# Attention and two feed-forward stages on one core: a port in the task order, low halves of weights by unit, conversions from unit index 3, earlier opening products

## Chip, core and metric

The kernel runs on one core of a Trainium2 chip. The metric is the device time of one execution in microseconds (us), from several runs; a profile shows one execution, engine by engine. The engines are called TensorE (PE; its weight loads are PEld), VectorE (DVE), ScalarE (ACT), GpSimd (POOL) and SyncE (SP, which issues the DMAs here).

## What is computed

```
attn = softmax(rot(q) @ rot(k).T / 8) @ v            # 2 batches, 8 heads, 576 x 64
x    = attn as (1152, 512)
x    = sum over e of p[:, e] * (relu(x @ w1[e]) @ w2[e])   # 4 experts, 512 -> 1024 -> 512
h    = x @ w_in;  out = max(0.01 * h, h) @ w_out           # 512 -> 2048 -> 512
```

All inputs and the output are fp32 in value; w_in and w_out reach the kernel as 64-bit words and are turned into fp32 by it.

## The kernel before

Products run in a reduced fp32 form: each operand is split into a rounded high half and the rest (low half), and three of the four products of halves are added. So each weight and each activation needs a rounding (`rounded`, L261) and a subtraction (`sub`, L908, recorded as L909).

The kernel has two parts, each with an order of instructions that a small list scheduler (`Plan`, L80) works out when the program is built: a task has a list of engines that may run it, a price on each, a rank, and the tasks it waits for. `Plan.order` goes through time, lets the engine that is free earliest take its ready task of lowest rank, and adds a lag for the signal; the instructions are issued in that order on each engine. `Plan({...})` gives the time at which each engine comes free from the part before. On the chip the engines run their queues in order and wait on semaphores, so the planned times set only the order.

The first part is attention, with half of the work of the first three units for block 0 mixed in. The second (from L843) runs twelve units of 512 hidden columns: units 0 to 7 are the four experts, two each; 8 to 11 are the second feed-forward stage. The 1152 tokens are two blocks: block 0 of 512, block 1 of 640. Units 0 to 2 (`AHEAD = 3`) have only block 1 left, the others both.

A unit has two stages. Stage 1 makes the hidden values by a seven-product scheme per quad (a block and a half of the columns): seven sums or plain quarters of the first matrix (`W1`, A11, A12, A22, S1 to S4, in `weights1`, L931) meet quarters, differences and sums of x (`x_sums`, `x_differences`, L983 to L995). Product 1 and product 5 open a quad, each in a bank of four called `start`; `seeded` (L1039) copies a bank into the next by ScalarE (L1042), `add_fifth` (L1045) adds product 5 by VectorE, and `hidden` (L997) empties a bank: high half on ScalarE (L1003), low half on VectorE (L1004). Unit 0 uses plain products (`stage1_whole`, L1013, recorded as L522). Stage 2 multiplies the hidden values by the second matrix (`W2`, `weights2`, L960), twelve matmuls for each tile of 128 tokens (L467), in a `start` bank, and VectorE adds the result to `acc` (L542, L545). Behind unit 7, `turned` (L1104) transposes `acc` into the x of the second stage, and its quarters and differences are split (L1098 to L1100).

Weights come in by `load_w` (L922) through three raw buffers of 512 KB, in turn. `converted` (L966) turns one piece of w_in or w_out (32 pieces, to be used from unit 8 on) into fp32: a load into one of two `wide` buffers, two steps on ScalarE (L974, L975), two on VectorE (L976, L977), one on GpSimd (L978), one on VectorE (L979), and a store to `narrow`. Pieces are ranked by planned time, 32 in 300 us, from unit 0 on.

Today the low halves and sums of weights may go to VectorE or GpSimd, whichever comes free first with a handicap; high halves to ScalarE or GpSimd.

Of the kernel before, what the change touches and what calls it, by code (L numbers as in the profile page):

```python
# [11 lines left out]
F32 = mybir.dt.float32  # L12
# [8 lines left out]
P = 128  # L21
# [9 lines left out]
HOLD = 3.5  # L31
# [36 lines left out]
LAG = {"PE": 0.2, "ACT": 0.16, "DVE": 0.19, "POOL": 0.12, "SP": 0.65, "DMA": 2.4}  # L68
# [11 lines left out]
class Plan:  # L80
# [18 lines left out]
    def order(self):  # L99
        free, ready, done, order, missing = dict(self.start), {}, {}, [], list(self.missing)  # L100

        def arrive(i):
            for e, us, more in self.tasks[i][1]:
                ready.setdefault(e, []).append((at[i], self.tasks[i][2] + more, i, us))

        at = [0.0] * len(self.tasks)
# [3 lines left out]
        while len(order) < len(self.tasks):  # L110
# [10 lines left out]
            _, _, i, us = min((x for x in ready[e] if x[0] <= t), key=lambda x: (x[0], x[2]) if e == "DMA" else x[1:3])  # L121
# [35 lines left out]
def attention_then_two_ffns(ctx, tc, xqk, vp, rope, dprob, w1, w2, w_in, w_out, out):  # L157
# [464 lines left out]
    with tc.manual_schedule():  # L622
# [230 lines left out]
        raw = [raw_p.tile([P, 2, FU], F32, name=f"raw{i}") for i in range(3)]  # L853
# [5 lines left out]
        wide = [cv_p.tile([P, FU, 2], I32, name=f"wide{i}") for i in range(2)]  # L859
# [8 lines left out]
        plan = Plan({"ACT": 7.5, "DVE": 12, "PE": 11})  # L868
        written, read = {}, {}

        def do(fn, choices, rank, reads=(), writes=(), also=()):
# [7 lines left out]
            t = plan.add(fn, [(c[0], c[1], c[2] if len(c) > 2 else 0) for c in choices], after, rank)  # L879
# [9 lines left out]
        def moved(fn, kb, rank, reads=(), writes=()):  # L889

            t = do(lambda e: fn(), [("SP", 0.48)], rank, reads, writes)
            d = plan.add(lambda e: None, [("DMA", kb / 260, 0)], [t], rank)
            for s in reads:
                read[s].append(d)
            for s in writes:
                written[s] = [d]
            return d

        def on(n, **more):
            return [(e, {"ACT": 0.15 + n / 1200, "DVE": 0.13 + n / 960}[e], x) for e, x in more.items()]  # L900

        def pair(n, **more):
            return [(e, {"DVE": 0.1 + n / 960, "POOL": 0.2 + n / 465}[e], x) for e, x in more.items()]

        def round_(n, **more):
            return [(e, {"ACT": 0.15 + n / 1200, "POOL": 0.2 + n / 1180}[e], x) for e, x in more.items()]
# [4 lines left out]
        def halves(name, hi, lo, x, n, rank, reads, slot, first=None, second=None):  # L911

            do(lambda e: rounded(e, hi, x), round_(n, **(first or {"POOL": 0, "ACT": 2})), rank, reads, [slot])
            do(sub(lo, x, f32(hi)), pair(n, **(second or {"POOL": 0, "DVE": 3})), rank, list(reads) + [slot], [slot])

        spin = {"raw": 0, "start": 0, "g": 0, "fifth": 0}

        def turnof(what, n):
            spin[what] += 1
            return (spin[what] - 1) % n  # L920

        def load_w(u, which, rank):  # L922
            rs = []
            for j in range(2):
                r = turnof("raw", len(raw))
# [3 lines left out]
            return rs  # L929

        def weights1(u, due):  # L931
# [5 lines left out]
            use = {"first": {"ACT": 0, "POOL": 0}, "second": {"POOL": 0, "DVE": 0}} if whole_ else {"first": {"ACT": 0, "POOL": 1}}  # L937
# [22 lines left out]
        def weights2(u, due):  # L960
            rs = load_w(u, 1, due)
            for c in range(NC):
                x = raw[rs[c // 2]][:, c % 2]
                halves(f"w2_{c}", W2[c][:, 0], W2[c][:, 1], x, 512, due + .5 * c, [("raw", rs[c // 2])], ("w2", c))

        def converted(i, due):  # L966
# [5 lines left out]
            w = ("wide", k)  # L972
            moved(lambda: sp.dma_start(raw_.rearrange("p f w -> p (f w)"), wide_weights(j, which)[:, c]), 512, due - 12, (), [w, ("low", k)])
            do(lambda e: act.activation(t, low.bitcast(U32), AF.Copy, scale=2.0 ** -29), [("ACT", 0.65)], due, [w, ("low", k)], [("rest", k)])  # L974
            do(lambda e: act.activation(s, high.bitcast(F32), AF.Square), [("ACT", 0.65)], due, [w], [("sq", k)])  # L975
            do(lambda e: dve.tensor_scalar(low, high, 3, 0x3FFFFFFF, op0=ALU.logical_shift_left, op1=ALU.bitwise_and), [("DVE", 0.85)], due, [w], [("low", k)])  # L976
# [232 lines left out]
```

## Time and profile before

| | us |
|---|---|
| median of 3 runs | 785.78 (785.42 to 786.85) |
| the profiled execution | 783.96 |
| its span, first to last instruction | 782.10 |
| TensorE busy in it | 734.7 (94%) |
| VectorE busy | 552.9 (71%) |
| GpSimd busy | 458.2 (59%) |
| ScalarE busy | 395.1 (51%) |

Times in the rows count from the first instruction of the profiled execution. The page splits the span into 40 slices of 19.6 us, with a digit for the busy tenths of each engine. A matmul's end is modelled, and successive ones overlap, so a group's duration is a little longer than the distance to the next group; distances are used for prices.

### The profile page before, as it was taken

The numbers are of one execution on the slowest core, as the hardware profiler recorded it, in microseconds if no ns is written. First come the engines' busy times: TensorE is split into PE (matmuls) and PEld (weight loads), VectorE is DVE, ScalarE is ACT, GpSimd is POOL, SyncE is SP. The second block draws the span as 40 slices with busy tenths as digits, with TensorE's granted clock in tenths as the row PEclk, the third lists the DMA queues.
The fourth block names the chain that finished last, engine by engine and source line by source line (L and its number), as shares of the span: only waits on it lengthen the run. The fifth ranks groups of instructions, "written<-read, shape, count | busy, mean of one in ns | idle before, by whom it ended". The sixth has DMA issues, their size and how long they took to land.

```text
span 782.1 us, 12238 instructions
## 1 busy us (share of the span) xinstructions
PE 734.7 (94%) x4396; PEld 658.2 (84%) x4396; DVE 552.9 (71%) x914; ACT 395.1 (51%) x964; POOL 458.2 (59%) x452
## 2 busy tenths in 40 slices
PE   6789899999998789599999999999997999999998
PEld 6678778888887678589898998989887889898997
DVE  6998977788758999977698785735569546264442
ACT  5688885766544464447263562504336427063450
POOL 7877957655249978748365383412558618265340
PEclk9999999999999999999999999999998999999999
DMA  8666645544024562555464543201101101020002
GB/s 264 173 199 154 156 109 130 165 120 106 14 96 135 136 215 80 162 183 168 148 180 142 167 151 115 96 27 55 54 1 55 54 30 52 27 78 5 1 28 95
DMA packets 40813, 84.57 MB, mean 108 GB/s; under 512 B 4656, under 2 KB 9520, under 8 KB 40752
## 3 DMA queue, kind: packets, MB, share of 16 engines
q1 hardware_dynamic: 39936, 83.00, 35.6%
q10 hardware_dynamic: 816, 0.79, 0.3%
q8 instruction: 35, 0.57, 0.3%
q14 instruction: 26, 0.21, 0.1%
HBM read 60.64 MB, written 10.75 MB: 91 GB/s over the span
## 4 chain that ended last, share of the span: by engine, by line
PE 72%; DVE 14%; POOL 5%; issue 3%; DMA 3%; ACT 2%; SPq 1%; POOLq 0%; ACTq 0%; DVEq 0%
PE start L467 30%; PE seeded L515 15%; PE start L515 10%; PE hy L467 4%; PE hp L588 4%; PE s L307 3%; PE o L467 3%; PE t L390 2%; DVE w L909 2%; DVE tmp L909 2%; DMA x<-in_xqk_dram 2%; DVE nm L324 1%; DVE pt L419 1%; POOL tmp L909 1%; DVE wide L977 1%
## 5 line engine op out<-in xcount | busy, mean ns | idle before, releaser
L467 PE MATMUL start<-w,h 128*128 128x512 f32 (+1 forms) x1164 | 269.8, 389 | 5.9 <-DVE h L1004 5.9
L467 PEld LDWEIGHTS start<-w,h 128*128 128x128 f32 x1164 | 215.1, 188 | 49.7 <-DVE h L1004 7.1
L515 PE MATMUL seeded<-xT,w 128*128 128x320 f32 (+1 forms) x480 | 74.9, 307 | 12.5 <-ACT seeded L1042 12.5
L515 PEld LDWEIGHTS seeded<-xT,w 128*128 128x128 f32 x480 | 70.3, 198 | 14.2 <-ACT seeded L1042 13.5
L978 POOL TENSOR_TENSOR rest<-wide,rest 128x512 int32<-128x512 int32 x32 | 45.2, 1413 | 61.1 <-DVE wide L977 27.2
L545 DVE SCALAR_TENSOR_TENSOR acc<-start,prob,acc 128x512 f32<-128x512 f32 x55 | 41.1, 748 | 54.4 <-PE start L467 54.3
L515 PE MATMUL seeded<-xt,w 128*128 128x320 f32 (+1 forms) x480 | 74.7, 302 | 0.0
L265 POOL TENSOR_SCALAR w<-raw 128x512 fp32r<-128x512 f32 x38 | 28.0, 737 | 78.7 <-PE start L467 67.9
L515 PE MATMUL start<-xT,w 128*128 128x320 f32 (+1 forms) x480 | 73.4, 298 | 0.1
L515 PEld LDWEIGHTS seeded<-xt,w 128*128 128x128 f32 x480 | 69.6, 194 | 0.9 <-ACT seeded L1042 0.3
L515 PEld LDWEIGHTS start<-xT,w 128*128 128x128 f32 x480 | 67.5, 190 | 1.5 <-DVE g L1009 0.3
L415 ACT ACTIVATE pt<-t 128x384 fp32r<-128x384 f32 (+2 forms) x128 | 53.4, 440 | 26.0 <-PE t L390 22.9
L909 POOL TENSOR_TENSOR h<-g,h 128x256 fp32r<-128x256 f32 (+1 forms) x64 | 55.2, 883 | 19.2 <-ACT h L1010 19.1
L419 DVE TENSOR_TENSOR pt<-t,pt 128x384 fp32r<-128x384 f32 (+2 forms) x128 | 60.1, 491 | 8.8 <-ACT pt L415 7.2
L1042 ACT ACTIVATE seeded<-start 128x320 f32<-128x320 f32 (+1 forms) x40 | 16.0, 399 | 93.4 <-PE start L515 40.8
L307 PE MATMUL s<-stk 128*128 128x288 f32 x288 | 53.3, 315 | 8.2 <-ACT p L334 5.4
L909 POOL TENSOR_TENSOR w<-raw,w 128x512 fp32r<-128x512 f32 x39 | 58.5, 1506 | 3.4 <-ACT w L263 2.4
L334 ACT ACTIVATE p<-s,nm 128x576 f32<-128x576 f32 x72 | 53.3, 740 | 12.8 <-DVE nm L324 12.2
L909 DVE TENSOR_TENSOR w<-raw,w 128x512 fp32r<-128x512 f32 x46 | 51.2, 1142 | 7.4 <-ACT w L263 5.2
L324 DVE TENSOR_REDUCE nm<-s 128x1 f32<-128x576 f32 x72 | 53.6, 749 | 3.9 <-PE s L307 3.1
L549 DVE TENSOR_TENSOR acc<-start,acc 128x512 f32<-128x512 f32 (+1 forms) x28 | 18.8, 673 | 51.7 <-PE start L467 51.7
L390 PE MATMUL t<-ident,p 128*128 128x128 f32 x288 | 45.6, 276 | 9.5 <-ACT p L334 3.7
(140 smaller groups left out, 1450.2 us busy)
## 6 DMA issues: line engine op xcount, KB each, us to landing
raw<-in_w_dram SPq DMA_DIRECT2D x32, 512.0 KB, 3.8
wide<-in_w_in_dram SPq DMA_DIRECT2D x16, 512.0 KB, 4.4
narrow<-rest SPq DMA_DIRECT2D x32, 256.0 KB, 4.0
wide<-in_w_out_dram SPq DMA_DIRECT2D x16, 512.0 KB, 3.8
raw<-narrow SPq DMA_DIRECT2D x16, 512.0 KB, 3.7
x<-in_xqk_dram SPq DMA_DIRECT2D x14, 576.0 KB, 6.6
stk<-hl SPq DMA_DIRECT2D x28, 288.0 KB, 5.5
hraw<-in_w_dram SPq DMA_DIRECT2D x12, 512.0 KB, 4.2
```

Source lines behind the costliest of these rows:

```text
L307: pe.matmul(sc[:, c, :HS], lhsT=l, rhs=r[:, c * HS:(c + 1) * HS], start=(k == 0), stop=(k == len(ops) - 1))
L324: dve.tensor_reduce(out=NM[n], in_=SC[n][:, :, :HS], axis=AX.XY, op=ALU.max, negate=True)
L334: act.activation(PP[p, i][:, h].rearrange("p (c k) -> p c k", c=2), SC[n][:, :, :HS], AF.Exp, bias=NM[n], accum_out=SM[p][:, col:col + 1])
L390: pe.transpose(t[:, j], flat[:, b * P:(b + 1) * P], ident)
L415: act.activation(hi, src, AF.Copy)
L419: dve.tensor_tensor(out=lo, in0=src, in1=f32(hi), op=ALU.subtract)
L467: pe.matmul(ps, lhsT=l, rhs=r, start=(k == 0), stop=(k == len(ops) - 1))
L515: pe.matmul(out, lhsT=W1[a][:, l, c, fs], rhs=x_of(g, b, r, c), start=first and (c, k) == (0, 0), stop=(c, k) == (1, 2), skip_group_check= ...
L545: dve.scalar_tensor_tensor(out=acc, in0=ps, scalar=prob[:, t, e:e + 1], in1=acc, op0=ALU.mult, op1=ALU.add)
L588: pe.matmul(HP[v, f], lhsT=w[:, c, l, f * P:(f + 1) * P], rhs=x[:, r, c], start=(c, k) == (0, 0), stop=(c, k) == (NC - 1, 2))
L909: return lambda e: eng[e].tensor_tensor(out=o, in0=a, in1=b, op=op)
L978: do(lambda e: pool.tensor_tensor(out=t, in0=low, in1=t, op=ALU.add), [("POOL", 1.45)], due, [w, ("low", k)], [("rest", k)])
```

## The change

- `Plan.order` knows a resource "port": a task that is marked (all two-input operations between buffers on VectorE and GpSimd, GpSimd's roundings, the conversion's steps) starts no earlier than the last marked task ended. Tasks that are free at the start count from -15 us, and SyncE and the DMA engines are free from there. A pseudo-engine "X" marks when the last attention results for block 1 are there (8.5 us).
- Low halves and sums of weights run on VectorE alone in units 0 to 3, 8 and 9 (`ON_DVE`), on GpSimd alone in the others; unit 0's first matrix keeps its choice. High halves of weights run on ScalarE alone.
- Two more raw buffers take the place of the two `wide` ones; units 0 to 2 and 8 to 11 load through all five, units 3 to 7 through three, and conversions use the other two.
- Conversions are added from unit index 3 on, eight per unit in units 3 to 6.
- Products 1 and 5 of the next unit's first quad are added ahead of stage 2 of the unit before, with a rank 3 us into it (behind unit 7: after its stage 2); the bank of product 1 is held until product 2 has been added to it, and the other tiles use the remaining banks. `HOLD` for the last tile is 0.
- The sums of x for block 1 run on GpSimd, those for block 0 on VectorE; differences and low halves of x on VectorE, high halves on ScalarE. For the second stage they are ranked in the order in which products need them.

The core of the diff:

```diff
-HOLD = 3.5
+HOLD = 0
+EARLY = 3
+ON_DVE = (0, 1, 2, 3, 8, 9)
...
+            for e, us, more, *port in self.tasks[i][1]:
+                ready.setdefault(e, []).append((at[i], self.tasks[i][2] + more, i, us, any(port)))

+        at = [-15.0] * len(self.tasks)
...
+            if port:
+                t = max(t, free.get("port", 0.0))
+                free["port"] = t + us
...
-        raw = [raw_p.tile([P, 2, FU], F32, name=f"raw{i}") for i in range(3)]
+        raw = [raw_p.tile([P, 2, FU], F32, name=f"raw{i}") for i in range(5)]
+        wide = [r.bitcast(I32).rearrange("p c f -> p (c f)").rearrange("p (f w) -> p f w", w=2) for r in raw[3:]]
...
-        wide = [cv_p.tile([P, FU, 2], I32, name=f"wide{i}") for i in range(2)]
...
-        plan = Plan({"ACT": 7.5, "DVE": 12, "PE": 11})
+        plan = Plan({"POOL": 0.0, "ACT": 7.5, "DVE": 12, "PE": 11, "SP": -15.0, "DMA": -15.0})
...
+            return [(e, {"DVE": 0.16 + n / 960, "POOL": 0.2 + n / 465}[e], x, True) for e, x in more.items()]
+            return [(e, {"ACT": 0.2 + n / 1200, "POOL": 0.2 + n / 1180}[e], x, e == "POOL") for e, x in more.items()]
...
-            do(lambda e: rounded(e, hi, x), round_(n, **(first or {"POOL": 0, "ACT": 2})), rank, reads, [slot])
-            do(sub(lo, x, f32(hi)), pair(n, **(second or {"POOL": 0, "DVE": 3})), rank, list(reads) + [slot], [slot])
+            do(lambda e: rounded(e, hi, x), round_(n, **(first or {"ACT": 0})), rank, reads, [slot])
+            do(sub(lo, x, f32(hi)), pair(n, **(second or {"DVE": 0})), rank, list(reads) + [slot], [slot])
...
+        held = set()
+
         def turnof(what, n):
+            while (what, spin[what] % n) in held:
+                spin[what] += 1
             spin[what] += 1
             return (spin[what] - 1) % n
...
-                r = turnof("raw", len(raw))
+                r = turnof("raw", 5 if u < AHEAD or u >= 2 * E else 3)
...
+        def LOW(u):
+            return {"DVE": 0} if u in ON_DVE else {"POOL": 0}
...
-            use = {"first": {"ACT": 0, "POOL": 0}, "second": {"POOL": 0, "DVE": 0}} if whole_ else {"first": {"ACT": 0, "POOL": 1}}
+            use = {"first": {"ACT": 0, "POOL": 0}, "second": {"POOL": 0, "DVE": 0}} if whole_ else {"second": LOW(u)}
...
-                    do(sub(t[o], x, y, f), pair(n, POOL=0, DVE=0.5), due + i, reads, [("tmp", o)])
+                    do(sub(t[o], x, y, f), pair(n, **LOW(u)), due + i, reads, [("tmp", o)])
...
-                halves(f"w2_{c}", W2[c][:, 0], W2[c][:, 1], x, 512, due + .5 * c, [("raw", rs[c // 2])], ("w2", c))
+                halves(f"w2_{c}", W2[c][:, 0], W2[c][:, 1], x, 512, due + .5 * c, [("raw", rs[c // 2])], ("w2", c), second=LOW(u))
...
+        LATE = {B11: 0, T1: 1, T2: 2, B21: 3, T3: 4, B22: 5, T4: 6}
+        XD = [4, 8]
...
+                do(sub(tmp[2 * k + h][:, :, :n], f32(x_block(g, i, 0)), f32(x_block(g, i, 1)), ALU.add), pair(2 * n, **({"POOL": 0} if g else {"DVE": 0})), due, [("x", g, i)], [("tmp", 2 * k + h)])
...
-                do(sub(t[o], t[x], t[y]), pair(2 * n, DVE=0, POOL=0), due, slots, [("tmp", 2 * o[0] + o[1])])
+                do(sub(t[o], t[x], t[y]), pair(2 * n, DVE=0), due + LATE[i] * (due > 100), slots, [("tmp", 2 * o[0] + o[1])])
...
-            seq, state = [(0, 1), (0, 5)], {}
+            seq = []
+            return products_of(u, quads, seq, now)
+
+        state = {}
+
+        def products_of(u, quads, seq, now):
...
+                    if m == 1:
+                        held.add(("start", i))
+                if m == 2:
+                    held.remove(st[1][1])
...
+                    x_differences(g, now + XD[g])
...
+        for c in (B11, T3, B21, B22):
+            d = plan.add(lambda e: None, [("X", 0.0 if c in (B11, T3) else 8.5, 0)], [], -99)
+            written["x", 1, c] = [d]
...
+            if u == AHEAD - 1:
+                x_sums(0, T)
+                x_differences(0, T)
             if u + 1 < NU:
                 weights1(u + 1, T + st2 - 12)
-            if u < 2 * E:
-                upto = convs if u == 2 * E - 1 else int(convs * (T + st2) / 300)
-                for i in range(done, min(upto, convs)):
+                nxt = [(g, j) for g in UNITS[u + 1][1] for j in range(2)]
+                if u != 2 * E - 1:
+                    products_of(u + 1, nxt, [(0, 1), (0, 5)], T + EARLY)
+            if AHEAD <= u < 2 * E:
+                upto = min(convs, convs * (u - AHEAD + 1) // (2 * E - AHEAD - 1))
+                for i in range(done, upto):
                     converted(i, T + st2 * (i - done + 1) / max(1, upto - done))
-                done = max(done, min(upto, convs))
+                done = upto
             T = stage2_tiles(u, gs_, T)
+            if u == 2 * E - 1:
+                products_of(u + 1, nxt, [(0, 1), (0, 5)], T)
             if u + 1 < NU:
                 nx = sum(7 * 6 * (HALVES[g] / 2400 + .0135) * 2 for g in UNITS[u + 1][1])
                 weights2(u + 1, T + nx - 8)
```

## Rows read from the trace of the kernel before

**Rows 1.** The page: TensorE's busy tenths in 40 slices of the span.

```profile
PE   6789899999998789599999999999997999999998
```

**Rows 2.** Stretches: length; PE, PEld, DVE, ACT, POOL busy; clock; DMA share; GB/s.

```profile
240.75:344.70 103.95, 86.21 (x451) 76.00 (x451) 95.44 (x113) 47.62 (x98) 81.88 (x57) 0.97 0.49 147
...
341.24:388.18 46.94, 46.94 (x277) 42.66 (x276) 34.79 (x58) 23.91 (x53) 28.31 (x22) 1.00 0.51 154
...
582.95:610.58 27.63, 23.53 (x158) 22.53 (x156) 24.21 (x34) 17.45 (x45) 20.54 (x19) 0.88 0.17 57
```

**Rows 3.** TensorE in order of time: start, us, line, operation, idle before.

```profile
324.31 3.46 PE L515 MATMUL seeded<-xT,w 128*128 128x320 f32 x12 [5.47 <-ACT seeded L1042]
...
358.46 1.92 PE L515 MATMUL seeded<-xT,w 128*128 128x320 f32 x12
...
369.12 19.23 PE L467 MATMUL start<-w,h 128*128 128x512 f32 x84
...
394.51 1.60 PE L515 MATMUL seeded<-xT,w 128*128 128x256 f32 x12
...
599.15 2.93 PE L515 MATMUL seeded<-xT,w 128*128 128x256 f32 x12 [3.55 <-ACT seeded L1042]
```

**Rows 4.** TensorE's waits (total, times, longest): from 220 us, then from 341.24.

```profile
PE seeded L515 <- ACT seeded L1042: 12.5, 4, 5.5
...
PE start L467 <- DVE h L1004: 5.9, 3, 3.2
...
PE seeded L522 <- POOL w L909: 1.8, 2, 1.3
...
PE start L515 <- DVE acc L545: 1.3, 1, 1.3
...
PE seeded L515 <- ACT seeded L1042: 3.9, 2, 3.6
```

**Rows 5.** VectorE, then GpSimd, in order of time in unit 2.

```profile
314.93 5.08 DVE L909 TENSOR_TENSOR w<-raw,w 128x512 fp32r<-128x512 f32 x3
...
331.59 0.67 DVE L909 TENSOR_TENSOR w<-raw,w 128x512 fp32r<-128x512 f32 x1
...
332.19 0.68 DVE L977 SCALAR_TENSOR_TENSOR wide<-wide 128x512 int32<-128x512 int32 x1
...
314.80 1.27 POOL L909 TENSOR_TENSOR w<-raw,w 128x512 fp32r<-128x512 f32 x1
...
344.86 1.30 POOL L909 TENSOR_TENSOR w<-raw,w 128x512 fp32r<-128x512 f32 x1
```

**Rows 6.** The same stretch, lines 909, 976, 977 and 979 alone (VectorE, GpSimd).

```profile
240.75:344.70 103.95, 43.11 (x34) 56.89 (x36) 0.97 0.49 147
...
240.75:344.70 103.95, 10.87 (x11) 0.97 0.49 147
...
240.75:344.70 103.95, 13.20 (x11) 0.97 0.49 147
...
240.75:344.70 103.95, 8.79 (x10) 0.97 0.49 147
```

**Rows 7.** GpSimd in unit 3: S1's low half for unit 4.

```profile
361.91 1.30 POOL L909 TENSOR_TENSOR w<-tmp,w 128x512 fp32r<-128x512 f32 x1
```

**Rows 8.** Units 3 to 7 by line (busy, mean ns); then one undisturbed step.

```profile
L978 POOL TENSOR_TENSOR rest<-wide,rest 128x512 int32<-128x512 int32 x22 | 30.2, 1373 | 54.6 <-DVE wide L977 24.0 <-ACT seeded L1042 12.6 <-issue 6.5
...
L909 POOL TENSOR_TENSOR w<-raw,w 128x512 fp32r<-128x512 f32 x16 | 22.5, 1407 | 2.6 <-ACT w L263 2.0
...
L979 DVE SCALAR_TENSOR_TENSOR rest<-sq,rest 128x512 f32<-128x512 f32 x22 | 21.6, 982 | 2.6 <-POOL rest L978 2.5
...
L977 DVE SCALAR_TENSOR_TENSOR wide<-wide 128x512 int32<-128x512 int32 x22 | 17.5, 796 | 0.2
...
L976 DVE TENSOR_SCALAR wide<-wide 128x512 int32<-128x512 int32 x21 | 10.6, 506 | 0.4 <-ACT rest L974 0.3
...
386.33 0.42 DVE L976 TENSOR_SCALAR wide<-wide 128x512 int32<-128x512 int32 x1
```

More of the change, by code (lines that the diff above doesn't have):

```diff
@@ L64 @@
 HALVES = [n // 2 for _, n in BLOCKS]
-LAG = {"PE": 0.2, "ACT": 0.16, "DVE": 0.19, "POOL": 0.12, "SP": 0.65, "DMA": 2.4}
+LAG = {"PE": 0.2, "ACT": 0.16, "DVE": 0.19, "POOL": 0.12, "SP": 0.65, "DMA": 2.4, "X": 0.0}
 def late(n):
@@ L119, in order @@
             t, e = best
-            _, _, i, us = min((x for x in ready[e] if x[0] <= t), key=lambda x: (x[0], x[2]) if e == "DMA" else x[1:3])
+            _, _, i, us, port = min((x for x in ready[e] if x[0] <= t), key=lambda x: (x[0], x[2]) if e == "DMA" else x[1:3])
+            if port:
+                t = max(t, free.get("port", 0.0))
+                free["port"] = t + us
             free[e] = t + us
@@ L878, in do @@
                 after.update(read.get(s, ()))
-            t = plan.add(fn, [(c[0], c[1], c[2] if len(c) > 2 else 0) for c in choices], after, rank)
+            t = plan.add(fn, choices, after, rank)
             for s in reads:
@@ L971, in converted @@
             low, high = raw_[:, :, 0], raw_[:, :, 1]
[L972 to L976, printed above, removed]
@@ L977, in converted @@
-            do(lambda e: dve.scalar_tensor_tensor(out=low, in0=high, scalar=-0x40000000, in1=low, op0=ALU.bitwise_and, op1=ALU.bitwise_or), [("DVE", 1.0)], due, [w], [("low", k)])
-            do(lambda e: pool.tensor_tensor(out=t, in0=low, in1=t, op=ALU.add), [("POOL", 1.45)], due, [w, ("low", k)], [("rest", k)])
-            do(lambda e: dve.scalar_tensor_tensor(out=f32(t), in0=s, scalar=MIN_HIGH ** 2, in1=f32(t), op0=ALU.is_ge, op1=ALU.mult), [("DVE", 1.0)], due, [("sq", k)], [("rest", k)])
+            w = ("raw", 3 + k)
@@ new lines, in converted @@
+            moved(lambda: sp.dma_start(raw[3 + k].bitcast(I32).rearrange("p c f -> p (c f)"), wide_weights(j, which)[:, c]), 512, due - 12, (), [w, ("low", k)])
+            do(lambda e: act.activation(t, low.bitcast(U32), AF.Copy, scale=2.0 ** -29), [("ACT", 0.65, 0)], due, [w, ("low", k)], [("rest", k)])
+            do(lambda e: act.activation(s, high.bitcast(F32), AF.Square), [("ACT", 0.65, 0)], due, [w], [("sq", k)])
+            do(lambda e: dve.tensor_scalar(low, high, 3, 0x3FFFFFFF, op0=ALU.logical_shift_left, op1=ALU.bitwise_and), [("DVE", 0.5, 0, True)], due, [w], [("low", k)])
@@ new lines, in converted @@
+            do(lambda e: dve.scalar_tensor_tensor(out=low, in0=high, scalar=-0x40000000, in1=low, op0=ALU.bitwise_and, op1=ALU.bitwise_or), [("DVE", 0.7, 0, True)], due, [w], [("low", k)])
+            do(lambda e: pool.tensor_tensor(out=t, in0=low, in1=t, op=ALU.add), [("POOL", 1.35, 0, True)], due, [w, ("low", k)], [("rest", k)])
+            do(lambda e: dve.scalar_tensor_tensor(out=f32(t), in0=s, scalar=MIN_HIGH ** 2, in1=f32(t), op0=ALU.is_ge, op1=ALU.mult), [("DVE", 0.7, 0, True)], due, [("sq", k)], [("rest", k)])
@@ L1019, in stage1_whole @@
                 x = [("x", g, v) for v in ((B11, B21), (T3, B22))[h]]
-                do(lambda e, f=f, h=h, b=b: whole(g, f, h, b), [("PE", us)], now, [("w1", A_OF[f // 2, k]) for k in range(2)] + x, [s])
+                do(lambda e, f=f, h=h, b=b: whole(g, f, h, b), [("PE", us, 0)], now, [("w1", A_OF[f // 2, k]) for k in range(2)] + x, [s])
                 now += us
@@ L1035, in stage1 @@
                 us = 6 * (n / 2400 + 0.0135)
-                st = state.setdefault(q, {})
+                st = state.setdefault((u, q), {})
                 def seeded(name, of, due):
@@ L1054, in stage1 @@
                 a, x = PRODUCTS[m]
-                do(lambda e, m=m, g=g, j=j, b=b: product(g, j, m, b, m in (1, 5)), [("PE", us)], now, [("w1", a), ("x", g, x)], [s])
+                do(lambda e, m=m, g=g, j=j, b=b: product(g, j, m, b, m in (1, 5)), [("PE", us, 0)], now, [("w1", a), ("x", g, x)], [s])
                 now += us
@@ L1099, in stage2_tiles @@
                         t = 2 * j[0] + j[1]
[L1100 to L1101 removed]
+                        halves(f"x{x}", x_block(g, x, 0), x_block(g, x, 1), tmp[t][:, :, :n], 2 * n, now + XD[g] + LATE[x], [("tmp", t)], ("x", g, x))
+                    x_differences(g, now + XD[g])
             return now
@@ L1136, in attention_then_two_ffns @@
         T = 11.0
-        for b_, blk in enumerate(BLOCKS):
-            for i in range(7):
-                written["x", b_, i] = []
         for u, gs_ in UNITS:
+            quads = [(g, j) for g in gs_ for j in range(2)]
             if u == 0:
```

27 lines of the change are left out of this document (7 added, 20 removed).

## Prediction

> **What bounds the kernel now.** I read the forty slices of the page first [rows 1]. TensorE is at eight or nine tenths nearly everywhere behind the attention part; it falls to 7 and 5 in the slices around 280 and 320 us and to 7 around 590 us. Elsewhere the expert stage is bound by TensorE itself, so only the holes can be won. Next I read the busy time by stretch [rows 2]: from the first product of unit 0 (240.75 us) to the last tile of unit 2 (344.70 us) there are 103.95 us with VectorE busy for 95.44 and GpSimd for 81.88; unit 3 behind it (341.24 to 388.18) has TensorE busy all the time. The hole of the second feed-forward stage is 582.95 to 610.58.
>
> What should units 0 to 2 take? The undisturbed prices stand in the timeline of TensorE [rows 3]: seven tiles of the second matrix end 19.06 us after they begin (the next product starts at 388.18, where the unit's stretch ends), 2.72 each; a product of 320 columns is half of the 1.76 us between the row at 358.46 and its successor, 0.88; one of 256 columns 0.72. Unit 0 has 16 such products' worth (eight times 12 matmuls, 14.1 us), units 1 and 2 have 14 each (12.3 us), and each has five tiles (13.6 us). That is 79.6 us, 80.3 with the product of unit 3 that is pulled in. So 103.95 - 80.3 = 23.7 us are lost here. The waits [rows 4] name 17.8 of them, since the list from 220 us on holds 12.5 + 5.9 + 1.8 + 1.3, of which 3.9 lie behind 582 us: waits for ScalarE's seed copies (L1042) and for VectorE's low halves of the hidden values (L1004). The other 6 us are columns at the lower clock behind a wait: the twelve matmuls at 324.31, behind a wait of 5.47, took 3.46 us against 1.92 [rows 3]; the granted clock of the stretch is 0.97, a part of it at 1.2 instead of 2.4 GHz. The last hole is alike: 27.63 - 23.53 = 4.1 idle, and at clock 0.88 the twelve matmuls at 599.15 took 2.93 against 1.60; some 7.3 us in all.
>
> The waits end on VectorE: ScalarE's seed copies wait for a bank that VectorE has not yet emptied. Why VectorE is late is seen at 314.93 [rows 5]: three low halves took 5.08 us, 1.69 each, while GpSimd ran its own two-input operations (1.27 for the one at 314.80); at 331.59, with GpSimd idle, one took 0.67, and the next operation started 0.60 later. The two engines take turns.
>
> **The change part by part.** *Conversions out of units 0 to 2.* In this stretch they cost VectorE 10.87 + 13.20 + 8.79 = 32.9 us [rows 6], and GpSimd 11 additions. All 32 now come from unit index 3 on, eight per unit. Each also issues a load and a store on SyncE; in units 3 to 6 these stand among the weight loads as those of seven conversions do today, with the DMA engines at a share of 0.51 [rows 2]: no cost there, and a shorter queue before the weight loads of units 0 to 2.
>
> *Weight splits.* Seventy two-input operations (splits, sums, differences; L909) ran here: 34 on VectorE in 43.11 us, 36 on GpSimd in 56.89 [rows 6]. Afterwards GpSimd keeps the four sums of block 1 and at most the splits of unit 0; some 65 to 70 go to VectorE. With GpSimd silent they cost 0.61 each, 43 us: twice the work in the time of today. With the other work, 95.44 - 43.11 - 32.9 = 19.5, VectorE has 62 us to do in 80: it fits, at 78%. If they stayed at today's 43.11 / 34 = 1.27 each, it would be 89 + 19.5 = 108, longer than the stretch is now. I take 0.61, the row with GpSimd idle, because that is the state which the change makes.
>
> *High halves on ScalarE alone* (0.63 each, for ten that GpSimd rounded), while 22 conversion steps leave it: ScalarE's 47.62 us [rows 2] get smaller. No cost; the cover is its idle half.
>
> *Two more raw buffers* where the wide ones lay: loads of units 0 and 1 no longer queue on SyncE behind a buffer in use, nor behind the wide loads. The tiles behind them move by 8 KB, so the first splits wait for other attention tiles. No row prices that; between a gain of the 1.8 us that TensorE waits now for GpSimd's first low halves [rows 4] and a loss of as much. I take a gain of 1.3, because the order of GpSimd no longer begins with sums whose inputs come late (the placeholder tasks in the plan).
>
> *Opening products.* Products 1 and 5 of the next unit are ranked 3 us into stage 2 instead of at its end, and the hold of the last tile goes. This adds a wait: the bank of product 1 is kept, three banks are left for the tiles, and in program order the third tile takes the bank of product 5; so from about 5.4 us into stage 2 TensorE's whole queue stands until S1 of the next unit is split and copied out. In unit 3 S1's low half was done at 363.2 [rows 7], before stage 2 got going at 369.12 [rows 3]: no cost in units 3 to 7. In units 0 and 1 there is time. In unit 2 the chain is long: W1 of unit 2, then twelve x operations of block 0 (the same temporaries), then S1: between the end of stage 1 of unit 1 and the third tile of unit 2 VectorE has some 26 us of work in 31. I leave 3 us of wait there (0 to today's 5.5).
>
> *Sum for units 0 to 2.* Of 23.7 us I leave 0.5 at the start, 1 at the first tile of unit 0, 1 in unit 1, 3 in unit 2, 1.5 for the clock behind them: 7. Gain 16.7.
>
> *The second stage's start.* Differences and splits of x go to VectorE and ScalarE only, in the order of need; unit 8 and 9 split on VectorE. GpSimd keeps the low halves of the hidden values, so the port is shared. I take a third of 7.3 us: gain 2.5 (from -2 to +5).
>
> *Conversions in units 3 to 6.* Today they already hold seven each without one wait of TensorE. Now eight, and all fifteen weight operations on GpSimd in units 4 to 6. Both engines together: (15 + 8) x 1.30 = 29.9 for GpSimd, at the price of the row at 344.86 [rows 5], 8 x (0.42 + 0.68 + 0.68) = 14.2 for VectorE's steps [rows 5, 8], 44.1 us of 46.94. It fits barely; cost 0.
>
> Sum: 16.7 + 2.5 = 19.2. The profiled execution took 783.96 us, its span 782.10; the median of the runs, 785.78, lies 1.8 above it. The differences are taken from the median: 766.6, say 766.5.
>
> **The rivals.** *VectorE stays the bound in units 0 to 2.* 78% on average is full in unit 2, and its queue is in order: one operation that waits for ScalarE holds up a hidden half behind it. For it: the holes today fall where VectorE is above 90%. Against it: the conversions are gone. Half of the gain would be left: 776 to 777. Chance 0.20.
>
> *The port becomes the bound in units 3 to 6*, on the other side. Its place is the split of S1 of the next unit on GpSimd, its point 5.4 us into stage 2. If an operation keeps today's mean under contention [rows 8], a unit needs 15 x 1.41 + 8 x 1.37 = 32.1 on GpSimd and 8 x (0.51 + 0.80 + 0.98) = 18.3 on VectorE, 50.4 us in 46.94. Four units then lose 3.5 each and 1.5 each for the clock as at 324.31, 20 us: it eats the gain, and with the second hole unimproved the time is 785.78 - 16.7 + 20 = 789. Against it: these means contain the time in which one engine waits for the other, so their sum counts it twice, and S1 was ready early [rows 7]. Chance 0.10.
>
> The Trainium skill, page "SBUF — State Buffer", section "Who interferes with whom", says that GpSimd and a VectorE operation with two SBUF inputs hold one port pair exclusively, each for its whole instruction. By that rule the 44.1 us of undisturbed times is the sum that counts, not the 50.4, and the rival falls short by 2.8 us a unit. The trace agrees with the rule at 314.93 (1.69 against 0.67), but no row shows a port booked to 94%.
>
> *The long operations have another cause*, so that the change doesn't do what it says: 108 us of VectorE in units 0 to 2, 4 more than the stretch has now: about 790. The row at 331.59 speaks against it. Chance 0.03.
>
> *The stalls move and the sum is nothing*: a wait for the early opener in each of units 0 to 2 instead of the seed copies: 785. Chance 0.07.
>
> **How the numbers follow.** Forecast 766.5 with 759 to 774: chance 0.55; all holes but the last gone, 757: 0.05; the first rival 0.20; the other three 0.20. The range 757 to 783 leaves out the last three; its upper end is the first rival with the bad ends of two unknowns (4.5 us at the second stage's start, 2 in unit 2). A measurement of this kernel can tell about 0.2% from no change, 1.6 us. Faster 0.80 (the first three), same 0.07, slower 0.13.
>
> **What would show it.** Right: no conversion before the stretch of unit 3; low halves on VectorE near 0.61 in units 0 to 2 with GpSimd almost empty; the last tile of unit 2 near 328 instead of 344.7; the waits for L1042 and L1004 below 6 us there. Wrong: low halves above 1 us with GpSimd idle; waits of opening products for weights at every unit's end; TensorE below nine tenths in units 3 to 6.

## The result and the profile after

| | before | after |
|---|---|---|
| median of the runs, us | 785.75 (785.42 to 786.85) | 761.87 (759.67 to 763.77) |
| ratio, 95% interval | | 0.9693 (0.9663 to 0.9722) |
| profiled execution, us | 783.96 | 759.67 |
| its span, us | 782.10 | 757.7 |

Faster by 23.9 us; the forecast was 766.5, a gain of 19.2. The profiled execution of after is the lowest of its four runs, so the two traces differ by 24.3 us.

The page of after, busy time and the forty slices, against [rows 1]:

```profile
PE 728.2 (96%) x4396; PEld 654.1 (86%) x4396; DVE 527.0 (70%) x927; ACT 422.0 (56%) x1017; POOL 385.9 (51%) x386
...
PE   6789899999999999999999999998999999999998
...
PEclk9999999999999999999999999999999999999999
```

The 7 and the 5 around 280 and 320 us are gone, and so is the 7 at 590; an 8 has come around 520 to 540 us. Sections 1 and 2 of the page say no more than that; the stretches tell how much. The columns are those of [rows 2]; the row of the stretch with fewer columns is line 914 alone (VectorE, GpSimd), the line that was 909:

```profile
240.37:323.71 83.34, 81.84 (x458) 73.97 (x456) 73.37 (x123) 43.72 (x89) 6.14 (x6) 1.00 0.33 104
414.00:461.00 47.00, 47.00 (x278) 42.72 (x277) 32.20 (x52) 23.65 (x54) 30.16 (x22) 1.00 0.44 142
461.00:508.00 47.00, 46.15 (x278) 42.02 (x277) 34.01 (x53) 26.05 (x59) 28.08 (x20) 1.00 0.50 164
561.00:590.00 29.00, 28.46 (x198) 26.91 (x197) 24.05 (x43) 23.43 (x61) 10.04 (x11) 1.00 0.12 37
...
240.37:323.71 83.34, 44.38 (x65) 2.03 (x2) 1.00 0.33 104
```

Units 0 to 2 took 83.34 us instead of 103.95, with one opening product more in them (0.72): 21.3 us. TensorE begins them 0.4 earlier. What is left of the 24.4 us between the spans, 2.7, came behind them. Line 914 on VectorE is 65 operations in 44.38 us, where there were 34 in 43.11 [rows 6]: nearly twice the work in the same time. These operations are the splits and sums of weights and also those of x. The granted clock of TensorE went from 0.97 to 1.00.

TensorE's waits of after, from 215 to 783 us, against [rows 4], and below them its timeline at the waits:

```profile
PE seeded L520 <- ACT seeded L1062: 3.4, 4, 1.5
PE hy L472 <- DVE acc L618: 1.4, 1, 1.4
PE start L520 <- POOL w L914: 0.9, 1, 0.9
PE start L520 <- DVE w L914: 0.6, 1, 0.6
```

```profile
283.18 1.14 PE L520 MATMUL seeded<-xt,w 128*128 128x320 f32 x6 [0.85 <-ACT seeded L1062]
...
308.76 0.74 PE L520 MATMUL start<-xT,w 128*128 128x256 f32 x4 [0.65 <-DVE w L914]
...
315.52 8.35 PE L472 MATMUL start<-w,h 128*128 128x512 f32 x36
323.71 0.88 PE L520 MATMUL seeded<-xt,w 128*128 128x256 f32 x6
...
480.06 0.74 PE L520 MATMUL start<-xT,w 128*128 128x256 f32 x4 [0.85 <-POOL w L914]
...
522.76 1.15 PE L520 MATMUL seeded<-xt,w 128*128 128x320 f32 x6 [0.53 <-ACT seeded L1062]
...
529.32 1.15 PE L520 MATMUL seeded<-xt,w 128*128 128x320 f32 x6 [1.50 <-ACT seeded L1062]
...
581.50 2.02 PE L520 MATMUL seeded<-xT,w 128*128 128x320 f32 x12 [0.51 <-ACT seeded L1062]
```

In units 0 to 2 two waits are left, 0.85 and 0.65 us, none of them for the hidden values, which cost 5.9 before. The last tile of unit 2 ends at 323.71. At the second stage's start 0.51 is left of the 3.55 and the clock's share behind it [rows 3], but three waits are new: 0.85 in unit 6, where product 1 of unit 7 stands for A11's low half from GpSimd (478.73 to 480.01 there), and 0.53 and 1.50 in unit 7. The 0.65 at 308.76 is of the same kind: product 1 of unit 3, for A11's low half from VectorE.

VectorE in unit 0 and GpSimd in units 0 to 2, in order of time, against [rows 5]:

```profile
258.06 0.68 DVE L914 TENSOR_TENSOR w<-raw,w 128x512 fp32r<-128x512 f32 x1
258.66 0.69 DVE L914 TENSOR_TENSOR w<-tmp,w 128x512 fp32r<-128x512 f32 x1
259.26 0.68 DVE L914 TENSOR_TENSOR tmp<-raw 128x512 f32<-128x512 f32 x1
```

```profile
234.85 6.25 POOL L914 TENSOR_TENSOR tmp<-xT 128x640 f32<-128x640 f32 x4
295.33 1.32 POOL L990 TENSOR_TENSOR rest<-raw,rest 128x512 int32<-128x512 int32 x1 [54.23 <-PE start L472]
305.38 1.38 POOL L990 TENSOR_TENSOR rest<-raw,rest 128x512 int32<-128x512 int32 x1 [8.74 <-DVE raw L989]
318.60 1.31 POOL L990 TENSOR_TENSOR rest<-raw,rest 128x512 int32<-128x512 int32 x1 [11.83 <-issue]
...
323.61 1.31 POOL L990 TENSOR_TENSOR rest<-raw,rest 128x512 int32<-128x512 int32 x1 [2.41 <-ACT w L268]
```

With GpSimd idle for 54 us, VectorE's two-input operations follow each other every 0.60 us, at 0.68 each. But L990 is GpSimd's step of a conversion: four of them ran in the stretch, where none was to run. The rank does not hold them, since an idle engine takes what is ready; these four and those behind them start when the raw buffers that they share with the loads of units 0 to 2 come free (their first load is issued at 278.4 us).

### The profile page after: what moved, and what is told of

It reads as the page before. It is cut to its first block, busy times and chain, and to the rows that moved or that the text cites. A ratio compares the mean times of both kernels' runs of the same rounds, so it can differ in the third digit from the quotient of the medians.

```text
span 757.7 us, 12165 instructions
## 1 busy us (share of the span) xinstructions
PE 728.2 (96%) x4396; PEld 654.1 (86%) x4396; DVE 527.0 (70%) x927; ACT 422.0 (56%) x1017; POOL 385.9 (51%) x386
## 4 chain that ended last, share of the span: by engine, by line
PE 85%; DVE 6%; POOL 3%; ACT 2%; DMA 2%; issue 1%; SPq 1%; ACTq 0%; POOLq 0%; DVEq 0%
PE start L472 35%; PE seeded L520 17%; PE start L520 12%; PE hp L593 4%; PE hy L472 4%; PE s L312 4%; PE o L472 3%; PE t L395 3%; PE seeded L527 1%; DVE pt L424 1%; DVE nm L329 1%; DMA x<-in_xqk_dram 1%; DMA tab<-in_rope_dram 1%; POOL x L232 1%; POOL hw L586 1%
## 5 line engine op out<-in xcount | busy, mean ns | idle before, releaser
L990 POOL TENSOR_TENSOR rest<-raw,rest 128x512 int32<-128x512 int32 x32 | 42.8, 1336 | 124.8 <-PE start L472 54.2
L268 ACT ACTIVATE w<-raw 128x512 fp32r<-128x512 f32 x81 | 50.3, 628 | 74.1 <-PE start L472 66.4
L914 POOL TENSOR_TENSOR w<-raw,w 128x512 fp32r<-128x512 f32 x46 | 64.0, 1401 | 41.0 <-ACT w L268 24.3
L520 PE MATMUL seeded<-xt,w 128*128 128x256 f32 (+1 forms) x480 | 74.3, 298 | 2.9 <-ACT seeded L1062 2.9
L520 PE MATMUL seeded<-xT,w 128*128 128x320 f32 (+1 forms) x480 | 71.4, 298 | 0.5 <-ACT seeded L1062 0.5
L520 PEld LDWEIGHTS seeded<-xT,w 128*128 128x128 f32 x480 | 67.2, 189 | 1.8 <-ACT seeded L1062 1.0
L312 PEld LDWEIGHTS s<-stk 128*128 128x128 f32 x288 | 41.6, 192 | 12.1 <-ACT p L339 7.9
L1062 ACT ACTIVATE seeded<-seeded 128x320 f32<-128x320 f32 (+1 forms) x80 | 32.0, 400 | 33.0 <-PE seeded L520 32.1
```

The lines of the kernel that those rows point to most:

```text
L268: act.activation(out, x, AF.Copy, scale=by)
L312: pe.matmul(sc[:, c, :HS], lhsT=l, rhs=r[:, c * HS:(c + 1) * HS], start=(k == 0), stop=(k == len(ops) - 1))
L520: pe.matmul(out, lhsT=W1[a][:, l, c, fs], rhs=x_of(g, b, r, c), start=first and (c, k) == (0, 0), stop=(c, k) == (1, 2), skip_group_check= ...
L914: return lambda e: eng[e].tensor_tensor(out=o, in0=a, in1=b, op=op)
L990: do(lambda e: pool.tensor_tensor(out=t, in0=low, in1=t, op=ALU.add), [("POOL", 1.35, 0, True)], due, [w, ("low", k)], [("rest", k)])
```

## The experiments

The theory to be tried: VectorE was late in units 0 to 2 because it and GpSimd wait for each other in two-input operations, and both moves (the splits to VectorE, the conversions out) are needed to end this. The rival: VectorE simply had too much to do, and it does not matter where the splits run once the conversions are out.

### One move undone

`splits_free` lets the weights' halves and sums run on either engine again, as before:

```diff
-            use = {...} if whole_ else {"second": LOW(u)}
+            use = {...} if whole_ else {"first": {"ACT": 0, "POOL": 1}, "second": {"POOL": 0, "DVE": 3}}
...
-pair(n, **LOW(u)), due + i
+pair(n, POOL=0, DVE=0.5), due + i
...
-("w2", c), second=LOW(u))
+("w2", c), {"POOL": 0, "ACT": 2}, {"POOL": 0, "DVE": 3})
```

> The changed kernel, with one part undone: low halves and sums of weights may run on VectorE or GpSimd and high halves on ScalarE or GpSimd, with the handicaps of before. All else stays. Port theory (GpSimd's two-input operations in units 0 to 2 hold up VectorE's): low halves on VectorE go from 0.68 to above 1.0 us on average there, GpSimd is busy for 30 us or more of units 0 to 2, waits of TensorE come back, 768 to 778 us. Rival (taking the conversions out of units 0 to 2 is what counts): 761 to 765.

Measured: 765.1 us (763.1 to 765.85), ratio 0.974 (0.9723 to 0.9757). That is near the rival's end. Units 0 to 2 have no hole, 82.22 us, though GpSimd runs 33 of their operations again. The median is 3.2 us above after's and the profiled execution 6.4 above; by the traces all of it arises behind unit 2, with one wait of 3.29 us in unit 6 as the largest.

`conv_early` ranks the conversions from unit 0 on, with the buffers for it (three for weights in every unit, two for conversions):

```diff
-                r = turnof("raw", 5 if u < AHEAD or u >= 2 * E else 3)
+                r = turnof("raw", 3)
...
-            if AHEAD <= u < 2 * E:
-                upto = min(convs, convs * (u - AHEAD + 1) // (2 * E - AHEAD - 1))
+            if u < 2 * E:
+                upto = convs if u == 2 * E - 1 else min(convs, int(convs * (T + st2) / 300))
```

> The changed kernel, with the conversions ranked by planned time from unit 0 on, as before, which also needs the three-buffer rotation for weight loads in all units. Theory that VectorE's total load in units 0 to 2 is the bound: some 9 to 13 conversions add 1.8 us each on VectorE alone and 1.3 on GpSimd; VectorE is full again, 772 to 782 us. Rival (the place of the splits is what counts, and a planner that knows the port fits the conversions in): 761 to 765.

Measured: 760.86 us (760.02 to 762.56), ratio 0.9693 (0.9677 to 0.9708): no loss, although seven conversions instead of four (eleven in the kernel before) ran before 324 us. TensorE's waits there are 1.97, 0.97, 0.42 and 0.28 us. So neither move is needed as long as the other is there.

`undo_both` is the two edits together:

> The changed kernel with both undone at once: low halves free to run on VectorE or GpSimd, high halves on ScalarE or GpSimd, and conversions ranked from unit 0 on (three raw buffers in turn). Theory that the two parts cover each other (either alone takes VectorE's sum in units 0 to 2 below the stretch): TensorE waits there again for 8 us or more, 772 to 784 us. Rival (neither matters; it is the start of the plan, the x part or the prices): 761 to 767.

Measured: 772.73 us (771.52 to 773.09), ratio 0.9841 (0.9824 to 0.9858): 10.9 us above after, where the two alone make +3.2 and -1.0. TensorE's timeline of `undo_both` in unit 2:

```profile
315.02 0.88 PE L520 MATMUL start<-xT,w 128*128 128x256 f32 x6
320.97 0.77 PE L520 MATMUL start<-xt,w 128*128 128x256 f32 x2 [5.07 <-ACT w L268]
323.66 1.22 PE L520 MATMUL start<-xt,w 128*128 128x256 f32 x4 [1.93 <-POOL w L914]
```

Product 5 of unit 3, the second opener, stands 5.07 + 1.93 us for the halves of S1, and the tiles of unit 2 behind it. This is the wait that the prediction priced at 3 us. In after product 5 (314.81) waits for nothing: it is harmless because the other edits make S1 early. So this run is not the old hole come back. Of its 13.4 us of waits in units 0 to 2, 10.7 are those of opening products, a part of the change that it keeps; on the loss of the kernel before, the runs of the next section tell more. And 12.1 of the 23.9 us stay won with both moves undone (10.8 between the profiled executions). From the first transposition behind unit 7 to the start of the last group of tiles its trace has 191.85 us, where the kernel before has 197.16: 5.3 us are won in the second stage, by other parts of the change. Another 3.8 are won in units 0 to 7, and 1.7 ahead of unit 0, where the runs differ by up to 3.2 us among themselves.

### One move alone, on the kernel before

`b_splits` moves the weights' low halves and sums to VectorE in units 0 to 3, 8 and 9, and nothing else:

```diff
+ON_DVE = (0, 1, 2, 3, 8, 9)
...
+        def LOW(u):
+            return {"DVE": 0} if u in ON_DVE else {"POOL": 0}
...
-            use = {...} if whole_ else {"first": {"ACT": 0, "POOL": 1}}
+            use = {...} if whole_ else {"first": {"ACT": 0}, "second": LOW(u)}
...
-pair(n, POOL=0, DVE=0.5), due + i
+pair(n, **LOW(u)), due + i
...
-("w2", c))
+("w2", c), {"ACT": 0}, LOW(u))
```

> The kernel before, with only the weight splits moved: low halves and sums on VectorE in units 0 to 3, 8 and 9, on GpSimd elsewhere, high halves on ScalarE. Theory that the two parts cover each other: conversions still take 33 us of VectorE's time or less, 766 to 776 us. Rival (conversions are what counts): 780 to 790, since VectorE then carries both.

Measured: 775.83 us (774.63 to 777.45), ratio 0.9885 (0.9862 to 0.9907): 9.0 us.

`b_conv_late` gives the conversions the ranks of after, and nothing else:

```diff
-            if u < 2 * E:
-                upto = convs if u == 2 * E - 1 else int(convs * (T + st2) / 300)
+            if AHEAD <= u < 2 * E:
+                upto = min(convs, convs * (u - AHEAD + 1) // (2 * E - AHEAD - 1))
```

> The kernel before, with only the conversions taken out of units 0 to 2 (eight per unit from unit index 3 on, with their own wide buffers). Theory that the two parts cover each other: most of the gain by itself, 764 to 772 us. Rival (the splits' place is needed): 778 to 786.

Measured: 782.71 us (780.76 to 784.53), ratio 0.9968 (0.9955 to 0.9982). It did not do what it was meant to: ten conversions still ran in units 0 to 2, since the rank is no due time. It says nothing on the theory, and much on the rank. So `b_gate` also makes each conversion's load wait for the fourth tile of unit 2:

```diff
-wide_weights(j, which)[:, c]), 512, due - 12, (), [w, ("low", k)])
+wide_weights(j, which)[:, c]), 512, due - 12, ["gate"], [w, ("low", k)])
...
+                        if u == AHEAD - 1 and i == 3:
+                            written["gate"] = [t_]
```

> The kernel before, with the conversions ranked late and their loads planned behind the fourth tile of stage 2 of unit 2, so that none runs in units 0 to 2 (ranked late alone, ten still ran there). Theory that either part alone takes VectorE below the stretch: 766 to 773 us. Rival (the splits' alternation on the two engines is the wait, conversions or not): 776 to 784.

Measured: 769.05 us (768.7 to 769.73), ratio 0.9802 (0.9787 to 0.9816): 15.5 us by the conversions alone. The stretch of units 0 to 2 in `b_gate`, all engines, then line 909 on VectorE and GpSimd:

```profile
241.44:327.86 86.42, 82.88 (x458) 73.86 (x458) 66.19 (x90) 33.52 (x71) 54.92 (x41) 1.00 0.31 98
...
241.44:327.86 86.42, 43.39 (x43) 43.43 (x27) 1.00 0.31 98
```

`b_splits_gate` is `b_splits` and `b_gate` together:

> The kernel before, with the weight splits moved as in the changed kernel and the conversions held as in the run beside it; start of the plan, port, opening products, raw buffers and x part stay as before. If these two parts carry the change: 762 to 768 us. If the rest of the change carries a share of its own in units 0 to 2: 769 to 775.

Measured: 767.79 us (766.75 to 768.83), ratio 0.9785 (0.977 to 0.9799). Two moves that give 9.0 and 15.5 alone give 16.8 together: for the most part they take the same loss away.

The stretches of units 0 to 2 (views by stretch; the mean is the busy time of the line of splits and sums by its count) side by side:

| kernel | conversions in it | splits and sums on VectorE: count, mean us | on GpSimd: count | VectorE busy, us | stretch, us |
|---|---|---|---|---|---|
| before | 11 | 34, 1.27 | 36 | 95.4 | 104.0 |
| `b_conv_late` | 10 | 35, 1.17 | 35 | 92.0 | 102.2 |
| `undo_both` | 8 | 31, 1.19 | 37 | 84.9 | 101.6 |
| `b_splits` | 9 | 51, 0.93 | 19 | 90.3 | 97.5 |
| `b_gate` | 0 | 43, 1.01 | 27 | 66.2 | 86.4 |
| `b_splits_gate` | 0 | 56, 0.79 | 14 | 66.7 | 84.9 |
| after | 4 | 65, 0.68 | 2 | 73.4 | 83.3 |
| `splits_free` | 4 | 36, 1.04 | 33 | 68.7 | 82.2 |

Two things are to be seen. From `b_gate` to `b_splits_gate` thirteen operations move to VectorE, and from `splits_free` to after 29, and VectorE's time for splits and sums goes only from 43.4 to 44.4 and from 37.6 to 44.4: what VectorE takes over it mostly gets back in shorter operations. And the stretch follows VectorE's sum: with 66 to 73 us it is 82 to 86 long, with 90 and more 97 to 104. `undo_both` is the exception, 84.9 and 101.6, because of the opening products that stand there (10.7 us); its stretch also holds two products more than that of after.

### Is it the waiting for each other?

What the table doesn't tell is whether GpSimd's work alone can make VectorE late. `pool_tt` puts idle additions on GpSimd in units 0 to 2 of after, three behind each high half of the hidden values, 72 in all; nothing waits for them:

```diff
+        def busy_pool(after):
+            for _ in range(3):
+                idle_last[0] = plan.add(lambda e: pool.tensor_tensor(out=gs[2], in0=gs[0], in1=gs[1], op=ALU.add), [("POOL", 0.0, 0)], [idle_last[0], after], 999.0)
...
+                if u < AHEAD:
+                    busy_pool(r_)
```

> The changed kernel, plus idle work on GpSimd in units 0 to 2: three additions of two 320-column tiles for each of the 24 hidden halves there, which nothing waits for, in the same order of all other engines. Port theory: 72 operations of about 0.9 us, 65 us of GpSimd; VectorE's low halves go from 0.68 to above 1.0 us, VectorE is full, TensorE's waits come back, 768 to 785 us. If the port costs VectorE nothing that matters: low halves stay near 0.7, 761 to 764 us.

`pool_set` puts fills in their place, which write as many columns and read nothing, 144 of them:

```diff
-            for _ in range(3):
-                ... pool.tensor_tensor(out=gs[2], in0=gs[0], in1=gs[1], op=ALU.add) ...
+            for _ in range(6):
+                ... pool.memset(gs[0], 0.0) ...
```

> The changed kernel, plus idle work on GpSimd in units 0 to 2 that only writes: six fills of one 320-column tile for each of the 24 hidden halves, in the same order of all other engines. If the additions of the run before cost their 19 us through the reads of two inputs from the buffers: VectorE's low halves stay near 0.68 us and the time at 760 to 765. If any GpSimd work on the buffers holds VectorE: low halves go up in proportion to the fills' busy time, 768 us or more.

Measured: `pool_tt` 780.83 us (779.82 to 781.76), ratio 0.9943 (0.9922 to 0.9964); `pool_set` 758.96 us (758.34 to 761.23), ratio 0.9679 (0.9658 to 0.97). GpSimd's additions as a group, the stretch, line 914 in it, and VectorE in order of time, in `pool_tt`:

```profile
L925 POOL TENSOR_TENSOR g<-g,g 128x320 f32<-128x320 f32 x72 | 86.1, 1197 | 5.3
...
241.99:345.38 103.39, 89.57 (x457) 79.84 (x456) 99.31 (x120) 43.56 (x89) 93.89 (x78) 0.92 0.25 77
...
241.99:345.38 103.39, 70.17 (x65) 3.68 (x3) 0.92 0.25 77
...
269.11 0.74 DVE L547 TENSOR_SCALAR acc<-start,prob 128x512 f32<-128x512 f32 x1
269.77 0.70 DVE L914 TENSOR_TENSOR tmp<-raw,tmp 128x512 f32<-128x512 f32 x1
270.40 1.37 DVE L914 TENSOR_TENSOR w<-tmp,w 128x512 fp32r<-128x512 f32 x1
271.69 1.36 DVE L914 TENSOR_TENSOR w<-raw,w 128x512 fp32r<-128x512 f32 x1
```

The same views of `pool_set`:

```profile
L925 POOL MEMSET g<- 128x320 f32 x144 | 53.0, 368 | 8.0
...
241.00:325.00 84.00, 82.99 (x469) 75.14 (x468) 74.84 (x124) 44.56 (x92) 60.93 (x150) 1.00 0.33 104
...
241.00:325.00 84.00, 45.76 (x66) 2.97 (x2) 1.00 0.33 104
...
257.73 0.68 DVE L914 TENSOR_TENSOR w<-raw,w 128x512 fp32r<-128x512 f32 x1
258.33 0.69 DVE L914 TENSOR_TENSOR w<-tmp,w 128x512 fp32r<-128x512 f32 x1
```

The same 65 operations took 44.38 us in after, 45.76 (66) beside 53 us of fills, and 70.17 beside 86 us of additions; the additions cost 19.0 us of time, the fills none. So GpSimd's two-input operations alone are enough to make a hole as long as the old one (103.39 us), and it is not that GpSimd is busy, but that it reads. Two limits: operations of GpSimd that read a single buffer were not tried, and the additions, 86 us, are more than GpSimd's own two-input work before (56.89 us in line 909 and 16.34 in line 978), so they show that this cause suffices, not that it made all of the old loss. VectorE's operations out of the matmul banks keep their price beside the additions: 0.74 at 269.11, as the 0.75 in after for the same line (mean of five).

### The other parts

`late_open` adds the opening products where they were, behind stage 2, and gives the last tile its hold again:

```diff
-HOLD = 0
+HOLD = 3.5
...
-                if u != 2 * E - 1:
-                    products_of(u + 1, nxt, [(0, 1), (0, 5)], T + EARLY)
...
-            if u == 2 * E - 1:
+            if u + 1 < NU:
                 products_of(u + 1, nxt, [(0, 1), (0, 5)], T)
```

> The changed kernel, with products 1 and 5 of the next unit back behind stage 2 in program order and rank, and the hold of 3.5 us for the last tile. Theory (the waits came from a late VectorE): 761 to 765 us. Rival (the opening products are what lets VectorE's lateness be covered): the seed copies are late again at each unit's start, 767 to 775.

Measured: 758.0 us (757.91 to 758.25), ratio 0.9654 (0.964 to 0.9668), the lowest of all kernels here. All of TensorE's waits in the same range of time:

```profile
PE hy L472 <- DVE acc L618: 1.4, 1, 1.4
PE seeded L520 <- ACT seeded L1062: 1.0, 2, 0.5
PE start L472 <- DVE h L1019: 0.2, 1, 0.2
```

6.3 us of waits have become 2.6: the waits at 283, 308, 480 and 522 us of after are gone, and the one at 529 is 0.51. The spans differ by 2.5 us, the medians by 3.9; the two intervals still touch, and `no_port` and `pool_set`, which keep the early products, have medians of 758.9 and 759.0, so the medians alone don't show a cost. The traces do: from the first product of unit 0 to the start of the last group of tiles it is 488.4 us here, 492.1 in after, 490.9 and 491.6 in those two. So the early opening products, with the missing hold, gave nothing here and cost some 2.4 to 3.6 us.

`no_port` leaves the port out of the planner's count:

```diff
-                ready.setdefault(e, []).append((at[i], self.tasks[i][2] + more, i, us, any(port)))
+                ready.setdefault(e, []).append((at[i], self.tasks[i][2] + more, i, us, False))
```

> The changed kernel, with the planner's port left out; prices, engines and ranks stay. If the order that the port gives is itself worth something: 766 to 774 us, with collisions in units 3 to 8. If it is the place of the work that counts: 761 to 764, since GpSimd is nearly empty in units 0 to 2 in either order.

Measured: 758.92 us (758.72 to 762.66), ratio 0.9681 (0.9654 to 0.9708): no different from after. What keeps the engines apart is where the tasks may run, not the count.

`old_start` takes back the free times at the start of the plan and the marks for the last attention results:

```diff
-        at = [-15.0] * len(self.tasks)
+        at = [0.0] * len(self.tasks)
...
-        plan = Plan({"POOL": 0.0, "ACT": 7.5, "DVE": 12, "PE": 11, "SP": -15.0, "DMA": -15.0})
+        plan = Plan({"ACT": 7.5, "DVE": 12, "PE": 11})
...
-            d = plan.add(lambda e: None, [("X", 0.0 if c in (B11, T3) else 8.5, 0)], [], -99)
+            d = plan.add(lambda e: None, [("X", 0.0, 0)], [], -99)
```

> The changed kernel, with the start of its plan as before: tasks free from 0 us instead of -15, no start times for GpSimd, SyncE and the DMA engines, and the x results of block 1 taken as there from the start. If the start carries a share: the first product waits again for GpSimd's low halves (1.8 us) and VectorE's order in unit 0 slips, 764 to 770 us. If not: 760 to 763.

Measured: 760.91 us (759.41 to 762.0), ratio 0.9696 (0.9679 to 0.9712): the waits for GpSimd's low halves at unit 0's first products are back (0.94 and 0.54 us), the one for `acc` (1.4) is gone, and the time is the same.

## Why the prediction was right, and where it was off

*What bounds the kernel.* The price list of units 0 to 2 (80.3 us with one opening product, 81.0 with two) holds: after took 83.34, of which 1.5 are listed waits and 0.8 is not assigned. The loss of 23.7 was real and nearly all of it could be won. One small slip: the waits that the prediction adds up come to 17.6 (21.5 less 3.9), not 17.8; TensorE's idle time in the stretch, 103.95 - 86.21, is 17.7.

*The cause.* "VectorE is late because the two engines take turns" is shown: `pool_tt` brings 19.0 us back by GpSimd's reads alone. But the prediction took both moves as needed and let the rival lose half the gain if VectorE stayed busy. The runs show one loss with two cures: VectorE's time in the stretch, which holds its waiting for GpSimd, has to go down, and the conversions alone do that (15.5 of 16.8). With 66 to 75 us (74.84 in `pool_set`) there is no hole, with 90 and more there is; where between them the limit lies was not measured, since `undo_both` (84.9) loses its time in another way.

*Weight splits at 0.61, "43 us".* Right: 65 in 44.38, a step every 0.60. *"VectorE has 62 us to do in 80, 78%."* It was 73.37 in 83.34, 88%. Of the 11 us too little, the splits make 1.4 and the four conversions that ran here 1.69 + 2.75 + 3.17 = 7.6; what is left, 21.4 against 19.5, is the rest of its work. At 88%, with almost no GpSimd beside it (6.14 us), it still caused only 1.5 us of waits: the first rival was right that VectorE stays nearly full, and wrong about what that costs.

*"All 32 come from unit index 3 on."* Wrong in detail: four came earlier. I read the edit of the rank as a due time; `b_conv_late`, with ten of eleven conversions where they had been, shows that it is none. In after the shared buffers do what the rank was credited with.

*The sum for units 0 to 2.* This is the term that was mis-sized. Of 23.7 I left 7; after leaves 2.3. The 3 us at unit 2's wait for S1 were none at product 5 and 0.65 at product 1, the 1.5 for the clock were nothing (granted clock 1.00), the 1 at the first tile was nothing. 16.7 was 21.3, and these 4.6 us are nearly the whole miss of 4.7.

*Opening products, "no cost in units 3 to 7".* Product 1 cost 0.85 in unit 6, for a low half on GpSimd. I had looked at product 5 and S1 alone, but product 1 is now issued ahead of the last products of stage 1 (480.06, with the first tile at 485.04), before A11's halves are there. `late_open` shows 2.4 to 3.6 in all.

*The port in units 3 to 6.* The rival fell, for the reason given. In after's stretch from 414 to 461 us, the groups of VectorE's conversion steps and GpSimd's splits:

```profile
L991 DVE SCALAR_TENSOR_TENSOR rest<-sq,rest 128x512 f32<-128x512 f32 x7 | 7.4, 1082 | 0.0
...
L989 DVE SCALAR_TENSOR_TENSOR raw<-raw 128x512 int32<-128x512 int32 x6 | 6.5, 1080 | 0.0
L988 DVE TENSOR_SCALAR raw<-raw 128x512 int32<-128x512 int32 x6 | 3.2, 538 | 0.1
...
L914 POOL TENSOR_TENSOR w<-raw,w 128x512 fp32r<-128x512 f32 x7 | 10.0, 1437 | 3.5 <-ACT w L268 3.3
```

The durations are as long as the rival feared or longer (1.08 where 0.68 is undisturbed). GpSimd's 30.16 and VectorE's 7.4 + 6.5 + 3.2 sum to 47.3 us in 47.0, yet TensorE is busy for 47.00. A sum of durations that hold the waiting counts it twice: in the timelines of the two engines these operations lie over each other for 10 us and cover only 37.6. The Trainium skill's rule of the exclusive pair (page "SBUF — State Buffer", section "Who interferes with whom") agrees with this stretch.

*The second stage's start.* Forecast 2.5; 2.7 came behind unit 2. The place itself gave far more: of 4.1 idle and the clock's share, 7.3 in all, 0.51 of idle time is left there. So this term was mis-sized too: it gave 6.7 (197.16 us against 190.47 from the first transposition to the last group of tiles). But 0.85 went to unit 6 and 2.03 to unit 7. About 1 us is not assigned. The number was near by luck.

*The start.* Forecast 1.3; TensorE begins the stretch 0.4 earlier and the 1.8 us of waits for GpSimd there are gone; `old_start` has 1.5 of them back and no other time. Since the runs differ by up to 3.2 us in where unit 0 begins, no run shows this term.

Open: after is 5.9 us faster than `b_splits_gate`, 7.2 between the profiled executions. The first transposition behind unit 7 and the last group of tiles, in after and then in `b_splits_gate`, place 5.4 of these in the second stage, 190.47 us against 195.87:

```profile
541.96 0.60 PE L1136 MATMUL start<-ident,acc 128*128 128x128 f32 x4
...
732.43 22.10 PE L472 MATMUL start<-w,h 128*128 128x512 f32 x108
...
543.71 0.60 PE L1118 MATMUL start<-ident,acc 128*128 128x128 f32 x4
...
739.58 22.10 PE L468 MATMUL start<-w,h 128*128 128x512 f32 x108
```

It is not the opening products (190.22 in `late_open`), the start of the plan (190.47 in `old_start`) or the two raw buffers (190.48 in `conv_early`, which goes without). The port's count may be a part (192.56 in `no_port`). What is left is the x part, its engines and its order, and the new prices of the planner; no run separates these.

## What to carry to other kernels

The duration of an operation in a trace holds its waiting for another engine: before moving work off a full engine, price it by the row in which the other engine is idle. Moving two-input operations from GpSimd to VectorE can cost VectorE little (here 6.8 us for 29 of them, 1.0 for 13), because the neighbours get shorter. And where two edits cure one loss, their gains alone do not add, so undo each of them and both; in a planner that lets a free engine take whatever is ready, a rank holds nothing back, only a dependence or a shared buffer does.

## What the hardware showed

GpSimd's fills, 144 of 320 columns at 0.368 us each, left VectorE's 128x512 low halves at 0.71 us (0.68 in after); additions of two tiles of the same width, 1.197 us each, took them to 1.15 (mean of 21). The Trainium skill states it so (page "SBUF — State Buffer", section "Who interferes with whom": VectorE with two SBUF inputs contends with a GpSimd instruction that reads SBUF, not with one that only writes), and these two runs agree. What I had not expected is the size: one engine's idle additions, whose results nothing uses, cost 19.0 us of a 762 us kernel.
